# Products of zeros in the gaps of the opening, and measured landing times for the first loads

## The chip, the cores and the metric

The kernel runs on one core of one Trainium2 chip. The metric is the device time of one execution in microseconds (us). Several executions are timed; one more is recorded by the hardware profiler, and all rows below come from that one.

## What is computed

The reference is a linear attention with the feature map elu(x) + 1, followed by a mixture of four small networks whose outputs are added with weights that depend on the row.

```
q, k, v: [8 batches, 8 heads, 576 positions, 64]      float32
phi(x) = where(x > 0, x, exp(x) - 1) + 1
kv  = sum over s of phi(k)[s, d] * v[s, e]             per batch and head
z   = sum over s of phi(k)[s, d]
x   = (phi(q) @ kv) / (phi(q) . z + 1e-6)              -> 4608 rows x 512
p   = domain_probs / sum(domain_probs)                 4608 x 4
out = sum over e of p[:, e] * (relu(x @ w1[e]) @ w2[e])
w1: [4, 512, 1024], w2: [4, 1024, 512]                 float32
```

## The kernel before, in words

**Tiling.** A batch has 576 positions: 512 are handled as a block of four chunks of 128, and the remaining 64 of each batch are gathered as "rest" rows. Heads are taken in pairs, so a batch has four pairs (pr = 0 to 3), each 128 columns of x. For each pair ScalarE takes the exponential (ek, L469), VectorE makes the feature map from it (kqp, L453 and L454), TensorE transposes phi(q) (L481), ScalarE copies the transpose to SBUF (qT, L494), TensorE sums phi(k) times v (L512, with the denominators beside it in L514, and the rest rows in L520), ScalarE casts that sum to SBUF (kvz, L531 and L532), TensorE multiplies by it (L545, denominators in L547), and VectorE divides (reciprocal L552, product L553, which writes x).

**Stages.** In the opening, which is batch 0, the products of the first expert cannot start before x exists. `turn_x` transposes the x of a pair on TensorE (L668), and ScalarE copies it to `xt0` (L673, shown in the profile by its buffer's name, s). The first layer of expert 0 (`first_l1` and `mm1`, L678) then runs as soon as pieces of it can: the 128-row slices of w1 are called dc, 0 to 3, slice dc needs x of pair dc, and four banks are accumulated in parallel so that each slice is used as it comes. Its second layer is `mm2` (L688). The other three experts follow for batch 0, with the attention of batch 1 between them. From about 82 us on, the 64 units of the remaining batches run in a form with seven products instead of eight per pair of half blocks (`l1_seven`, L832, and `l2_unit`, L908), which needs sums of weight blocks that VectorE makes (`sums_w1`, L630, and `sums_w2`, L651). While these run, the attention of later batches is computed ahead.

**What sets the order.** The class `Plan` collects all operations with an engine, a duration, a priority and the data keys they read and write. `Plan.order` lays them out once, then `deadlines` replaces the priority of every operation that is not on TensorE by the latest time at which it may start (`late`), and the operations are laid out again. `lay_out` models the engines and one shared stream of transfers: a transfer has a time to move (`move`), a lead before it and a landing time after it. POOL's operations keep the order in which they are written. The order of instructions in the program, and so in every engine's queue, is that of the second layout. The hardware's engines then work through their queues in that order, and semaphores hold them where data or a PSUM bank isn't free.

**Loads.** `load_pair` issues the k, v and q of a head pair and `load_rest` those of the rest rows, both through `dma` (L261). The first pair and the k and v of the first rest rows are issued on the SP queue, all that follows in the opening on POOL: the pairs 1 to 3, then w1 and w2 of expert 0 (`load_w1`, `load_w2`), then those of the other experts.

**PSUM banks that matter here.** l2b1 receives the transposes of phi(q) of the opening in its first half (the 16-bit view's 512 columns are 256 columns of 32 bits). l2b2 receives the sums and the denominators. l2b3 receives the transposes of x, and `at` the products L545. `identh` is the identity matrix for transposes, made on POOL; `qTr` are two buffers for the transposed rest rows that VectorE sets to zero at the start.

Of the kernel before, what the change touches and what calls it, by code (L numbers as in the profile page):

```python
# [20 lines left out]
class Plan:  # L21
# [37 lines left out]
    def deadlines(self):  # L59
        ops = self.ops  # L60
        late = [o["start"] if o["eng"] == "PE" else BIG for o in ops]
        for n in range(len(ops) - 1, -1, -1):
            o = ops[n]
            for d in o["deps"]:
                x = ops[d]
                lat = self.HOP if x["eng"] != o["eng"] or x["move"] else 0.03
                if x["move"]:
                    lat += x["lead"] + x["move"] + self.LAND
                late[d] = min(late[d], late[n] - lat - x["dur"])
        for n, o in enumerate(ops):  # L70
            if o["eng"] != "PE":
                o["pri"] = late[n]

    def order(self):
# [59 lines left out]
def kernel(  # L134
# [10 lines left out]
    nc = tc.nc  # L145

    B, H, S, D = q.shape
    N, E = moe_domain_probs.shape
    _, Dm, F = moe_w1.shape

    P = 128
    NT = 512
    C = NT // P
    R = S - NT
    DE = D + 1
    DC = Dm // P
# [2 lines left out]
    HD = Dm // 2  # L159
    FH = F // 2  # L160
    NJ = N // NT
    T0, TU = 79.0, 6.4

    pl = Plan()
# [5 lines left out]
    def sb(name, shape, dt):  # L170
        return pc.tile(shape, dt, tag=name, name=name)
# [29 lines left out]
    qTr = [sb(f"qTr{i}", [P, DC, P], FP16) for i in range(2)]  # L201
# [6 lines left out]
    identh = s15h[:, 0:P]  # L208
# [22 lines left out]
    l2b = [pp.tile([P, 512], FP32, tag=f"l2b{i}", name=f"l2b{i}") for i in range(4)]  # L231
# [6 lines left out]
    def rot(key, n):  # L238
        i = cnt.get(key, 0)
        cnt[key] = i + 1  # L240
        return i % n
# [5 lines left out]
    def stage_keys(i):  # L247

        if i < 2:
            return ("st", i, 0), ("st", i, 1), ("st", i, 2)  # L250
        return ("xp", 0), ("xp", 1), ("u2", 0)
# [4 lines left out]
    def dma(queue, pri, out_, in_, w, move, r=(), hold=None, mark=None, after=0.0):  # L256

        eng = {"POOL": nc.gpsimd, "SP": nc.sync, "ACT": nc.scalar}[queue]

        def go():  # L260
            i = eng.dma_start(out=out_, in_=in_)  # L261
            if mark:
                last[mark] = i.ins.name
            if hold:
                tc.add_manual_dep(
                    i.ins,
                    last[hold],
                    mybir.DependencyInfo(
                        mybir.DependencyClass.Sync, mybir.DependencyReason.DATA
                    ),  # L270
                    reason="load order",
                )

        pl.add(
            queue,
            0.72 if queue == "POOL" else 0.5,
            pri,
            go,
            r=r + ((("mark", hold),) if hold else ()),
            w=w + ((("mark", mark),) if mark else ()),  # L280
            move=move,
            after=after,
        )
# [3 lines left out]
    def v16(i):  # L287

        flat = vss[i].rearrange("p h c d -> p (h c d)").bitcast(FP16)
        return flat[:, 0 : 2 * C * D].rearrange("p (h c d) -> p h c d", h=2, c=C)  # L290

    def load_pair(b, pr, queue, pri, after=0.0, hold=None):
        hs = slice(2 * pr, 2 * pr + 2)
        n = 3 if b < 2 else 2
        i = rot("stage%d" % n, n) if n == 2 else rot("stage3", 3)
        stage[b, pr] = i
        kk = stage_keys(i)
        vo = vss[i] if b or queue == "SP" else v16(i)
        parts = [(k, kqs[i][:, 0], kk[0]), (v, vo, kk[2]), (q, kqs[i][:, 1], kk[1])]
        if b == 0:  # L300
            parts[1:] = parts[:0:-1]
        for t, o, key in parts:
            if (b, pr, key) == (0, 0, kk[1]):
                load_rest(0, "SP", 0, parts=(0,))
            keys = (key, "v00") if (b, key) == (1, ("st", 1, 2)) else (key,)
            dma(queue, pri, o, t[b, hs, 0:NT].rearrange("h (p c) d -> p h c d", c=C), keys, 0.7,
                hold="w" if b == 2 else hold if key == kk[0] else None,
                mark="k0" if (b, pr, key) == (0, 0, kk[0]) else None, after=after)

    def load_rest(b, queue, pri, after=0.0, parts=(0, 1, 2)):  # L310
        par = b % 2
        rs = slice(par * R, par * R + R)
        for i in parts:
            t, o = ((k, kqr[rs, 0]), (v, vr[rs]), (q, kqr[rs, 1]))[i]
            dma(queue, pri, o, t[b, :, NT:S].rearrange("h s d -> s h d"), (("str", par, i),), 1.1,
                hold="w" if b in (2, 3) else None, after=after)

    def load_w1(e, dcs):
# [455 lines left out]

    units = [(j, s, e) for j in range(1, NJ) for s in range(2) for e in range(E)]
    U = lambda n: T0 + n * TU

    def prep(n):

        j, s, e = units[n]  # L780
        xi, ti = n % 2, n % 3
        xp, xT = xp_b[xi], xT_b[ti]
        pri = U(n) - 7.0
        for c in range(2):
            cc = 2 * s + c
            if j < NJ - 1:
                src, ps = x_b[j % 2][:, cc, :], p_nat[:, j, cc, e : e + 1]
                r = [("x", j % 2, pr, cc) for pr in range(DC)] + ["pnat" if j > 1 else "pnat0"]
            else:
                src, ps = xr_sb[:, cc, :], p_rest[:, cc, e : e + 1]  # L790
                r = [("xr", b, pr) for pr in range(DC) for b in (2 * cc, 2 * cc + 1)] + ["prest"]
            pl.add("ACT", 0.6, pri, lambda c=c, src=src, ps=ps: nc.scalar.activation(  # L792
                xp[:, c, :], src, AF.Copy, scale=ps), r=r, w=(("xp", xi, c),))
        pl.add("SP", 1.25, pri + 1, lambda: nc.sync.dma_start_transpose(
            out=xT.rearrange("p c k t -> p (c k) t"), in_=xp.rearrange("p c d -> p (c d)")),
            r=(("xp", xi, 0), ("xp", xi, 1)), w=(("xT", ti),), move=1.5, lead=0.2)
# [100 lines left out]
    def l2_unit(n):  # L897
# [88 lines left out]
        r = (O(0), O(2))  # L986
        if j < NJ - 1:
            dma("SP", p0 + 9, out_t[j][:, 2 * s : 2 * s + 2, :], ot, (), 1.5, r=r)
# [5 lines left out]
    def consts(i):  # L994
        nc.vector.memset(vps[i][:, :, :, D:DE], 1.0 / SX)
        nc.vector.memset(vprs[i][(1 - i) * R : (2 - i) * R], 0.0)
        nc.vector.memset(vprs[i][i * R : (i + 1) * R, :, D:DE], 1.0 / SX)
# [5 lines left out]
    pl.add("DVE", 0.4, 5, lambda: [nc.vector.memset(kvs[i], 0.0) for i in range(4)],  # L1003
           w=(("kvz", 0), ("kvz", 1), ("kvz", 2), ("kvz", 3)))
    pl.add("DVE", 0.8, 20, lambda: consts(1), w=(("vp", 1), ("vpr", 1)))
    for i in range(2):
        pl.add("DVE", 0.27, 26 + 10 * i, lambda i=i: nc.vector.memset(qTr[i], 0.0),
               w=[("qTr", i, pr) for pr in range(DC)])
    load_pair(0, 0, "SP", 0)
    load_rest(0, "SP", 0, parts=(1,))  # L1010
    load_pair(0, 1, "POOL", 0, hold="k0")
    load_pair(0, 2, "POOL", 0)
    rest_maps(0, True, 3, (0,))
    for pr in range(DC):
        if pr == 3:
            load_pair(0, 3, "POOL", 0)
            load_w1(0, range(DC))
            probs(0, 2, p5_b, ("p5",), "pnat0", 24)
            load_w2(0)
            load_rest(0, "POOL", 0, parts=(2,))  # L1020
        attention(0, pr, True, 2.5 + pr, 0.4, two=True)
        turn_x(pr, 4.9 + pr)
# [34 lines left out]
    def batch(b):  # L1057

        due = U(8 * (b - 1)) - 8
        for pr in range(DC):  # L1060
# [6 lines left out]
                rest_maps(b, False, t - 2)  # L1067
            attention(b, pr, False, t, 1.5)

    prep(0)  # L1070
    prep(1)
    for n in range(nu):
# [9 lines left out]
    with tc.manual_schedule(  # L1082
        engines={
            mybir.EngineType.PE,
            mybir.EngineType.Activation,
            mybir.EngineType.DVE,
            mybir.EngineType.Pool,
            mybir.EngineType.SP,
        }
    ):  # L1090
        todo = pl.order()
        for o in todo:
            o["fn"]()


# [28 lines left out]
```

## Time and profile before

| | |
|---|---|
| median of 4 runs | 498.97 us (497.71 to 499.8) |
| the profiled execution's own time | 499.8 us |
| its span | 498.0 us |
| TensorE busy | 481.1 us of the span (97%) |
| VectorE busy | 408.7 us (82%) |
| ScalarE busy | 366.6 us (74%) |
| POOL busy | 41.6 us (8%) |
| granted TensorE clock, mean | 0.998 |

A row of the timeline gives the start in us, the busy time in us, the engine, the line of the kernel, the operation, what it writes and reads, the size and the number of instructions merged into the row; in brackets stands how long the engine was idle before it and what ended that. PE is TensorE, ACT is ScalarE, DVE is VectorE. A row of waits names the waiting engine, the line that waited, what it waited for, the sum of the waiting time, how often, and the longest. A row of the chain gives a start, a duration and what was working then; the chain is followed back from the last instruction of the program. [...] what the products themselves show of the speed of the array is read from how far apart they start.

### The profile page before, as it was taken

The numbers are of one execution on the slowest core, as the hardware profiler recorded it, in microseconds if no ns is written. First come the engines' busy times: TensorE is split into PE (matmuls) and PEld (weight loads), VectorE is DVE, ScalarE is ACT, GpSimd is POOL, SyncE is SP. The second block draws the span as 40 slices with busy tenths as digits, with TensorE's granted clock in tenths as the row PEclk, the third lists the DMA queues.
The fourth block names the chain that finished last, engine by engine and source line by source line (L and its number), as shares of the span: only waits on it lengthen the run. The fifth ranks groups of instructions, "written<-read, shape, count | busy, mean of one in ns | idle before, by whom it ended". The sixth has DMA issues, their size and how long they took to land.

```text
span 498.0 us, 14872 instructions
## 1 busy us (share of the span) xinstructions
PE 481.1 (97%) x6040; PEld 426.1 (86%) x6040; DVE 408.7 (82%) x1033; ACT 366.6 (74%) x690; POOL 41.6 (8%) x67
## 2 busy tenths in 40 slices
PE   2899999999999999999999999999999999999995
PEld 2544456999999999999999999999999999999995
DVE  5668998988998999899988899889988675757664
ACT  5547658988987798769876988789766767676641
POOL 7656700000000000000000000000000000000000
PEclk9999999999999999999999999999999999999999
DMA  8999969948685686574656755657633233334221
GB/s 227 196 233 220 263 147 192 210 107 177 125 159 120 169 164 140 128 170 113 173 120 153 153 154 118 166 142 125 159 54 74 57 86 34 97 44 77 54 44 43
DMA packets 125573, 67.11 MB, mean 135 GB/s; under 512 B 95520, under 2 KB 119600, under 8 KB 125504
## 3 DMA queue, kind: packets, MB, share of 16 engines
q1 hardware_dynamic: 116112, 51.79, 48.4%
q0 software_dynamic: 9232, 14.10, 13.8%
q8 instruction: 47, 0.77, 0.7%
q10 hardware_dynamic: 160, 0.26, 0.1%
q14 instruction: 22, 0.18, 0.1%
HBM read 45.16 MB, written 9.44 MB: 110 GB/s over the span
## 4 chain that ended last, share of the span: by engine, by line
PE 93%; DMA 2%; ACT 2%; POOL 1%; DVE 1%; issue 0%; DVEq 0%
PE l1b L832 40%; PE l2b L908 38%; PE l1b L678 6%; PE l2b L688 6%; PE at L568 2%; PE at L517 1%; DMA w<-in_moe_w_dram 1%; POOL kq L261 1%; DMA kq<-in_k_dram 1%; ACT xp L792 0%; DVE ot L972 0%; ACT h L846 0%; PE at L520 0%; PE l2b L481 0%; POOL vs L261 0%
## 5 line engine op out<-in xcount | busy, mean ns | idle before, releaser
L832 PEld LDWEIGHTS <-w 128*128 128x128 f16 x2048 | 133.4, 98 | 5.1
L846 ACT ACTIVATE h<-l1b 128x512 f16<-128x512 f32 x128 | 76.8, 600 | 53.7 <-PE l1b L832 48.5
L908 PE MATMUL l2b<-w,h 128*128 128x256 f16 x768 | 114.9, 273 | 0.0
L908 PE MATMUL l2b<-t,s 128*128 128x256 f16 x768 | 114.3, 273 | 0.0
L832 PEld LDWEIGHTS <-w1x 128*128 128x128 f16 x1536 | 100.1, 98 | 3.9 <-issue 0.2
L908 PEld LDWEIGHTS <-s 128*128 128x128 f16 x1024 | 90.9, 98 | 6.6
L852 DVE CUSTOM_DVE_ANT_0 h<-l1b,p 128x512 f16<-128x512 f32 x64 | 44.1, 690 | 45.3 <-PE l1b L832 42.0
L792 ACT ACTIVATE xp<-x,p_nat 128x512 f16<-128x512 f16 x112 | 77.6, 721 | 0.9 <-DMA kqr<-in_q_dram 0.2
L832 PE MATMUL l1b<-xT,w 128*128 128x128 f16 x1024 | 78.1, 219 | 0.0
L832 PE MATMUL l1b<-xs,w 128*128 128x128 f16 x1024 | 78.1, 219 | 0.0
L832 PE MATMUL l1b<-xs,w1x 128*128 128x128 f16 x1024 | 77.9, 219 | 0.1
L908 PEld LDWEIGHTS <-h 128*128 128x128 f16 x768 | 67.4, 98 | 4.5
L894 DVE TENSOR_TENSOR s<-h 128x512 f16<-128x512 f16 x128 | 53.9, 421 | 2.1
L849 ACT COPY l1b<-l1b 128x512 f32<-128x512 f32 x64 | 36.7, 574 | 12.4 <-PE l1b L832 11.7
L849 ACT COPY u<-l1b 128x512 f32<-128x512 f32 x64 | 37.5, 586 | 11.1 <-PE l1b L832 10.9
L852 DVE CUSTOM_DVE_ANT_0 h<-l1b,u 128x512 f16<-128x512 f32 x64 | 43.8, 684 | 1.1 <-PE l1b L832 0.4
L849 ACT COPY p<-l1b 128x512 f32<-128x512 f32 x64 | 37.4, 584 | 8.9 <-PE l1b L832 7.2
L810 DVE TENSOR_TENSOR xs<-xT,xs 128x256 f16<-128x256 f16 x128 | 36.8, 288 | 3.4
L469 ACT ACTIVATE ek<-kq 128x512 f16<-128x512 f32 x60 | 37.9, 632 | 2.2 <-DMA kq<-in_k_dram 1.6
L832 PE MATMUL l1b<-xT,w1x 128*128 128x128 f16 x512 | 39.0, 219 | 0.0
L908 PE MATMUL l2b<-w,s 128*128 128x256 f16 x256 | 38.4, 273 | 0.0
L454 DVE TENSOR_TENSOR kqp<-ek,kqp 128x512 f16<-128x512 f16 x64 | 27.2, 425 | 6.0 <-ACT ek L469 1.7
(125 smaller groups left out, 568.8 us busy)
## 6 DMA issues: line engine op xcount, KB each, us to landing
w<-in_moe_w_dram POOLq DMA_DIRECT2D x32, 256.0 KB, 8.1
out_dram<-ot SPq DMA_DIRECT2D x16, 512.0 KB, 2.9
kq<-in_k_dram SPq DMA_DIRECT2D x25, 256.0 KB, 3.2
kq<-in_q_dram SPq DMA_DIRECT2D x25, 256.0 KB, 3.1
vs<-in_v_dram SPq DMA_DIRECT2D x25, 256.0 KB, 3.9
kq<-in_k_dram POOLq DMA_DIRECT2D x5, 256.0 KB, 7.2
kq<-in_q_dram POOLq DMA_DIRECT2D x5, 256.0 KB, 6.1
xT<-xp SPq DMA_TRANSPOSE x64, 3.2
```

The costliest lines, as they stand in the source:

```text
L454: nc.vector.tensor_tensor(out=o, in0=ek[:, i], in1=o, op=AO.min)
L469: pl.add("ACT", 0.55, pri + i * step, lambda i=i: nc.scalar.activation(ek[:, i], kq[:, i], AF.Exp), r=(sk[i],), w=(("ek", ei, i),))
L678: nc.tensor.matmul(out=bank, lhsT=w1_sb[e][:, dc, fj * P : (fj + 1) * P], rhs=xt0[:, dc, :], start=(dc == 0), stop=(dc == DC - 1),)
L688: nc.tensor.matmul(out=bank, lhsT=hts[ht[fj]][:, c * P : (c + 1) * P], rhs=w2_sb[e][:, fj, :], start=(fj == 0), stop=(fj == FC - 1),)
L792: pl.add("ACT", 0.6, pri, lambda c=c, src=src, ps=ps: nc.scalar.activation(xp[:, c, :], src, AF.Copy, scale=ps), r=r, w=(("xp", xi, c),))
L810: lambda o=o, a=a, b_=b_: tt(out=o, in0=a, in1=b_, op=AO.subtract),
L832: nc.tensor.matmul(out=bank[:, fc * P : (fc + 1) * P], lhsT=wt[:, kc, fc * P : (fc + 1) * P], rhs=r[:, kc, :], start=(start and fc == 0 an ...
L846: return lambda: nc.scalar.activation(o, bank, AF.Relu)
L849: return lambda: nc.scalar.copy(o, bank)
L852: return lambda: nc.vector._custom_dve(TENSOR_ADD_SAT, out=o, in0=bank, in1=t, s0=BIG, s1=0.0)
L894: pl.add("DVE", 0.36, U(n + 1) + d - 0.5, lambda i=i, a=a, b_=b_, alu=alu: tt(out=s4[:, i], in0=a, in1=b_, op=alu), r=r, w=(Q(i),))
L908: nc.tensor.matmul(out=l2b[bank][:, half * HD : (half + 1) * HD], lhsT=a[:, c, :], rhs=w[:, c], start=(opens and first and c == 0), stop=( ...
```

## The change

The change has three parts.

First, a function `keep_warm` issues one product on TensorE: the identity against 256 columns of `qTr[0]`, which holds zeros, written to the second half of bank l2b1, where nothing reads it. When the finished order is turned into instructions, each gap that the planner's layout leaves on TensorE before 22 us (`WARM`) is filled with as many such products as fit at 0.115 us each, less 0.1 us; in the first gap 28 (`COLD`) fewer are issued. In the built program there are 78: 43, 15, 4, 2, 3, 3 and 8 in the gaps from the first to the last.

Second, the setting to zero of `qTr[0]` is moved out of the plan to an earlier place, so that it stands in VectorE's queue ahead of the clearing of `kvs`.

Third, the planner's model gets other times for moving the first transfers of batch 0: 0.7, 1.2 and 0.95 us for the three parts of the first pair on SP in place of 0.7 each, 0.72 for the pairs on POOL, and 1.8, 0.7 and 0.7 for the rest rows in place of 1.1. The five first loads get negative priorities, which `deadlines` now leaves as they are. These numbers are in the model alone; what they alter is the order in which the planner puts the instructions. In the built program the five loads keep their order. TensorE's order is the same, apart from the zero products, until about 84 us; VectorE's and ScalarE's differ in a few places from about 24 and 37 us on; after 84 us all orders differ in places.

```diff
@@ Plan.deadlines
-            if o["eng"] != "PE":
+            if o["eng"] != "PE" and o["pri"] >= 0:
                 o["pri"] = late[n]
...
+    WARM, COLD = 22.0, 28
     T0, TU = 79.0, 6.4
@@ load_pair
             if (b, pr, key) == (0, 0, kk[1]):
-                load_rest(0, "SP", 0, parts=(0,))
+                load_rest(0, "SP", -8, parts=(0,))
             keys = (key, "v00") if (b, key) == (1, ("st", 1, 2)) else (key,)
-            dma(queue, pri, o, t[b, hs, 0:NT].rearrange("h (p c) d -> p h c d", c=C), keys, 0.7,
+            pri += queue == "SP" and not b
+            dma(queue, pri, o, t[b, hs, 0:NT].rearrange("h (p c) d -> p h c d", c=C), keys,
+                0.72 if queue == "POOL" or b else (0.7, 1.2, 0.95)[parts.index((t, o, key))],
@@ load_rest
-            dma(queue, pri, o, t[b, :, NT:S].rearrange("h s d -> s h d"), (("str", par, i),), 1.1,
+            dma(queue, pri, o, t[b, :, NT:S].rearrange("h s d -> s h d"), (("str", par, i),),
+                1.1 if b else (1.8, 0.7, 0.7)[i],
@@ the start of the program
-    for i in range(2):
-        pl.add("DVE", 0.27, 26 + 10 * i, lambda i=i: nc.vector.memset(qTr[i], 0.0),
-               w=[("qTr", i, pr) for pr in range(DC)])
-    load_pair(0, 0, "SP", 0)
-    load_rest(0, "SP", 0, parts=(1,))
+    nc.vector.memset(qTr[0], 0.0)
+    pl.add("DVE", 0.27, 36, lambda: nc.vector.memset(qTr[1], 0.0),
+           w=[("qTr", 1, pr) for pr in range(DC)])
+    load_pair(0, 0, "SP", -9)
+    load_rest(0, "SP", -7, parts=(1,))
...
+    def keep_warm():
+
+        nc.tensor.matmul(out=l2b[1][:, 256:512], lhsT=identh,
+                         rhs=qTr[0][:, 0:2].rearrange("p a t -> p (a t)"), start=True, stop=True)
@@ issuing the order
         todo = pl.order()
+        free = 0.0
         for o in todo:
+            if o["eng"] == "PE" and o["start"] < WARM:
+                gap = o["start"] - free
+                for _ in range(int((gap - 0.1) / 0.115) - (COLD if free == 0.0 else 0)):
+                    keep_warm()
+                free = o["start"] + o["dur"]
             o["fn"]()
```

## The prediction

> **What bounds the kernel now.** I read the page's busy table and slices first, then TensorE's waits, the chain in order of time, and last the timeline of the first 30 us, where the change lies.
>
> ```profile
> PE 481.1 (97%) x6040; PEld 426.1 (86%) x6040; DVE 408.7 (82%) x1033; ACT 366.6 (74%) x690; POOL 41.6 (8%) x67
> PE   2899999999999999999999999999999999999995
> ```
>
> TensorE is busy 97% and only the first two slices (12.45 us each) and the last are not full.
>
> ```profile
> PE l2b L481 <- DVE kqp L454: 7.2, 1, 7.2
> PE l2b L512 <- ACT vs L463: 1.2, 1, 1.2
> PE l2b L668 <- DVE x L553: 1.1, 2, 0.7
> PE at L545 <- ACT kvz L532: 1.0, 1, 1.0
> PE l1b L678 <- ACT s L673: 0.7, 1, 0.7
> ```
>
> These are all of TensorE's listed waits in the whole run: 11.2 us, the last at 24.29. After that it is fed to the end, so whatever brings the product at 24.29 forward brings the end forward, as long as its inputs keep up. That chain, in order of time, is led by transfers up to 16.93 (the weights w1 of expert 0) and by TensorE from there.
>
> ```profile
> 10.57 6.36 DMA w<-in_moe_w_dram
> ...
> 18.75 0.85 PE l1b L678 x2
> 19.61 0.43 PE l2b L481 x4
> ...
> 25.35 3.61 PE l1b L678 x16
> ```
>
> Here is the prize. Two 128x512 products take 0.85 us at 18.75, 0.43 each; sixteen take 3.61 us at 25.35, some 0.22 each. The timeline shows the switch at 21.54: the pair of products L545 and L547 needs 0.133 us before it and 0.083 after. The row PEclk stands at 9 throughout, so it does not show this. From 16.97 to 21.54 TensorE works without a gap at half speed: 4.57 us that could take about half.
>
> [...] half rate, and 4.57 us from the start of unbroken work to the switch. [...] the reciprocal L552 of pair 0 had its own sums at 11.57 but started at 12.33, when products of the next pair into the same bank had ended at 12.23.
>
> **The change, part by part.**
>
> *The zero products.* The built program's order has 78 of them, each 128x256, into the unused half of bank l2b1: 43 ahead of the first transposes (L481), 15 ahead of pair 0's L545, 4 ahead of turn_x of pair 0 (L668), 2 ahead of pair 1's L545, 3 ahead of pair 2's transposes, 3 ahead of turn_x of pair 1, 8 ahead of the dc=3 products of L678. A 256-column product costs, by half of the 512-column rows, 0.213 us at half clock and 0.109 at full.
>
> Their start: identity (POOL, done at 1.31) and the memset of qTr0, which moves up behind the memset that ends at 2.25 and takes 0.27; so about 2.55.
>
> Clock release: I take the trace's own 4.57 us, giving 7.1. [...]
>
> Now walk the queue with 7.1. Of 43 products 21 or 22 run slow, the rest fast: 2.55 + 21.4 x 0.213 + 21.6 x 0.109 = 9.5 [...]. The first transposes stood at 7.19; they move to 9.5. What is queued behind: ScalarE's copy of qT, 9.43, goes to 9.96. The 15 products come next and wait, by the bank, for that copy to end: 10.6, plus 15 x 0.109 = 12.25. L545 of pair 0 stood at 10.90. So pair 0's products end 1.35 us late less what the faster clock gives back (9 pairs at 0.05 here); its reciprocal goes from 12.33 to 13.2. Behind it ScalarE casts kvz (two casts, 0.45 in all) and then copies qT of pair 1, 13.9 to 14.5, and the 4 products wait for that: 14.55 + 0.44, so turn_x of pair 0 goes from 13.32 to 15.0. Add 0.22 for its own transposes, 0.22 for 2 products, 0.33 for pair 1's L545 group and 0.38 plus 0.17 of drain for pair 2's sums, which share the bank: they end at 16.3 instead of 15.15. Reciprocal, casts and the copy qT of pair 2 follow (0.1 + 0.25 + 0.45 + 0.6): 17.7 instead of 16.54. Then 3 products, 0.33: turn_x of pair 1 goes from 16.25 to 18.1, and the first L678 0.22 later, from 16.97 to 18.3. **So TensorE enters the dense stretch 1.35 us late.**
>
> From there everything runs at full clock and the loss is made good: up to the transposes of pair 3 (L481, 19.40) the same queue of one product, pair 2's sums, pair 3's sums and two products took 2.45 us and takes 0.22 + 0.33 + 0.38 + 0.43 = 1.36, giving 19.7; L545 of pair 3 comes at 20.95 instead of 21.54; its reciprocal at 21.5 (22.17); turn_x of pair 3 at 22.55 (23.23); the copy L673 at 23.0 (23.65); the dc=3 products at 23.65 instead of 24.29. The 8 products ahead of them, 0.87 us, lie under that copy (0.42 us from transposes to its start, 0.59 of its own, 0.05 after), so cost nothing; without that cover they would cost all 0.87. Sum: **-0.65 us**. [...] With all products taken out of the way and a clock that is up, it gives 22.3 (-2.0), limited by the elementwise work of pair 3 and by the norms.
>
> *Do inputs keep up?* POOL's queue issues each load when the one eight before it has landed, so its rows tell landings: w1 of expert 0 complete by 20.97, w2 of it by 26.7, w1 of expert 1 by 31.95. Expert 1's first product stands at 33.98, its dc=3 one 0.65 later; a gain of up to 2.6 us meets no load. None of the early POOL loads waits for TensorE. VectorE is near its limit from 33.3 to 79 (its waits for TensorE there sum to 1.3 us), but that stretch begins with a wait for L688 at 33.32 and so moves with it. I cost this at nothing; if the cover fails, the gain is lost at 81.84, where the first seven-product unit needs x of batch 1.
>
> *The planner's landing times and the fixed early priorities.* The order of the SP queue's first five loads is the same, and so is ScalarE's up to 35 us and TensorE's (zero products apart) up to about 84. VectorE takes the sums of w1 ahead of the first sum of w2; w1 had landed at 20.97, w2's first half by 24.1, so that is neutral to good. From 84 on all orders differ in places. TensorE shows no listed wait after 84 now, and 64 units x 14 products x 0.44 plus 24 attention pairs x 0.57 make 408 of the 410.8 us from 81.84 to 492.67: a better order can give back at most 2.8, a worse one has no such floor. I take 0, with -1.0 to +1.0 as ends.
>
> *Sum.* -0.65 + 0 against the profiled execution: 499.8 us (span 498.0 and 1.8 around it) would be 499.15. That execution is the slowest of the four; the median is 498.97, and I apply the difference to it: 498.3.
>
> **The rivals.**
>
> 1. *Half a gain (main).* As worked out: 498.3, own range 497.2 to 499.7. For it: the waits by bank and the queue in front of the transposes. Chance 0.50.
> 2. *The whole gain.* The clock is up before 6 us and the bank waits are shorter, or the new order takes up some of the 2.8 us. 2.0 us: 497.0 (496.2 to 497.5). Against it: the three groups that wait for the qT copies have to slip. Chance 0.30.
> 3. *Slower: the clock comes late.* [...] the 43 and 15 products run at 0.213 us in front of real work. All 43 slow end at 11.7. Break-even is at a release of about 8.4, a loss of 1.5 us at about 11.5 (501 at 12.5), and with no release before real work is dense the walk ends near 29, that is 503.7. For it: from 14.7 to 18.1 TensorE was over 80% busy in the trace of before and the clock was not released at 18.1. Against: the stream is unbroken. Chance 0.12.
> 4. *It does what it says and nothing comes of it:* VectorE's stretch from 40 to 79 does not move, TensorE waits at 81.84; 498.9. Against: that stretch begins with a wait for TensorE. Chance 0.08.
>
> **How the numbers follow.** About 0.3% (1.5 us) is what a measurement of this kernel can tell from no change. Faster than that: rival 2, 0.30, and a tail of the main case, 0.02. Slower: rival 3 less its mild part, and a bad order after 84: 0.12. Within: 0.56. Eight in ten lie from 496.5 to 500.0: this leaves out most of rival 3 and the best of rival 2.
>
> **What would show each step.** Right: zero products from about 2.5; their spacing falls from 0.21 to 0.11 near 7; first transposes near 9.5; pair 0's L545 near 12.2, released by ScalarE; the first L678 near 18.3 and at 0.22 each; the dc=3 products near 23.65. Wrong: L678 at or before 17.0 (rival 2); spacing of 0.21 up to 11 or later (rival 3); a TensorE wait near 81 (rival 4); equal times at 84 but not at the end (the order).

## The result, and the profile after

The changed kernel is slower: 500.34 us median (499.41 to 503.38) against 499.35 for the kernel before (497.71 to 500.45), ratio 1.0022 with a 95% interval of 1.0017 to 1.0028. That is 0.85 to 1.4 us lost, where 0.65 us was to be gained, and 500.34 lies just outside the range on record. The profiled execution took 500.21 us, its span is 498.4 (before: 499.8 and 498.0).

Lines of the kernel after are four higher than before: L481 is L485, L545 is L549, L668 is L672, L678 is L682, L747 is L751, L832 is L836, L852 is L856, L908 is L912. L1076 is the zero products.

The row of TensorE from the page's slices, kernel after. It answers to the row that began with 28:

```profile
PE   7899999999999999999999999999999999999995
```

The first slice is fuller, but it is filled with zeros. TensorE's waits in the whole run, kernel after (engine, line, what it waited for, us, times, longest):

```profile
PE l2b L1076 <- DVE qTr L1010: 2.6, 1, 2.6
PE l2b L1076 <- ACT qT L498: 2.4, 3, 1.2
PE l1b L836 <- DVE h L856: 0.3, 1, 0.3
PE at L572 <- DVE x L585: 0.2, 1, 0.2
```

The waits of before's opening, 11.2 us, are gone from the list or taken over by zero products. What is new is the third row: a product of the steady part waits for VectorE. No such row stood in the list before. The timeline of TensorE in the opening, kernel after:

```profile
2.55 7.62 PE L1076 MATMUL l2b<-qTr,s 128*128 128x256 f16 x43 [2.55 <-DVE qTr L1010]
10.01 0.39 PE L485 MATMUL l2b<-s,kqp 128*128 128x128 f16 x4
...
11.07 1.80 PE L1076 MATMUL l2b<-qTr,s 128*128 128x256 f16 x15 [0.29 <-ACT qT L498]
...
15.02 0.60 PE L1076 MATMUL l2b<-qTr,s 128*128 128x256 f16 x4 [1.22 <-ACT qT L498]
...
18.22 0.49 PE L1076 MATMUL l2b<-qTr,s 128*128 128x256 f16 x3 [0.89 <-ACT qT L498]
18.54 0.39 PE L672 MATMUL l2b<-s,x 128*128 128x128 f16 x4
18.76 0.38 PE L682 MATMUL l1b<-s,w 128*128 128x512 f16 x1
...
24.13 0.81 PE L682 MATMUL l1b<-s,w 128*128 128x512 f16 x3
```

The change does what it says. Three products take 0.49 us and fifteen 1.80, so one costs 0.109 at full clock. The 43 took 7.62, which fits about 27 of them at 0.213: the clock was released near 8.2. The dense stretch starts late (18.76 for 16.97) and at full clock, and the dc=3 products of L682 start at 24.13 instead of 24.29.

From there both kernels run alike up to the first seven-product unit, at 81.69 after and 81.84 before. At the end TensorE has lost: its last product ends at 493.31 after and 492.67 before. So a lead of 0.15 us at 82 is a lag of 0.64 at the end, and the loss lies in the steady part. Measured from the first product that reads w1x (82.13 after, 82.29 before) to TensorE's end, **the steady part** is 411.17 us after and 410.38 before.

The largest single piece of it is near 86 us. TensorE there, kernel after:

```profile
85.52 0.61 PE L836 MATMUL l1b<-xT,w 128*128 128x128 f16 x8
86.48 0.61 PE L836 MATMUL l1b<-xs,w 128*128 128x128 f16 x8 [0.35 <-DVE h L856]
```

Eight such products otherwise start 0.45 us after the eight before them; here it is 0.96. They wait for VectorE's L856 to empty their bank. In the kernel before, nothing waits there:

```profile
85.49 0.60 PE L908 MATMUL l2b<-w,h 128*128 128x256 f16 x4
85.93 0.61 PE L832 MATMUL l1b<-xs,w1x 128*128 128x128 f16 x8
```

VectorE's timeline ahead of L852 (L856 after), first before, then after:

```profile
83.06 0.74 DVE L747 SCALAR_TENSOR_TENSOR ot<-l2b,p_nat,ot 128x512 f32<-128x512 f32 x1
83.72 0.41 DVE L810 TENSOR_TENSOR xs<-xT 128x512 f16<-128x512 f16 x1
84.06 0.74 DVE L747 SCALAR_TENSOR_TENSOR ot<-l2b,p_nat,ot 128x512 f32<-128x512 f32 x1
84.76 0.69 DVE L852 CUSTOM_DVE_ANT_0 h<-l1b,u 128x512 f16<-128x512 f32 x1
```

```profile
82.32 0.73 DVE L751 SCALAR_TENSOR_TENSOR ot<-l2b,p_nat,ot 128x512 f32<-128x512 f32 x1
82.98 0.41 DVE L375 TENSOR_SCALAR kqpr<-kqr 64x512 f16<-64x512 f32 x1
83.49 0.42 DVE L376 TENSOR_TENSOR kqpr<-ek,kqpr 64x512 f16<-64x512 f16 x1
83.83 1.40 DVE L751 SCALAR_TENSOR_TENSOR ot<-l2b,p_nat,ot 128x512 f32<-128x512 f32 x2
85.15 0.67 DVE L856 CUSTOM_DVE_ANT_0 h<-l1b,u 128x512 f16<-128x512 f32 x1
```

VectorE is idle for no more than 0.11 us at a time in either stretch; it is a matter of what is queued ahead. Counted over the program, the new order puts one L751 more (0.73 us) and one pair L375 and L376 more (0.83) ahead of the first L856, and one L814 less (0.41). That makes 1.15 us. About 0.6 of it fell into idle time that VectorE still had in the kernel before, in gaps of 0.49 and 0.48 us ahead of its instructions at 78.14 and 80.75. The rest stayed: L856 starts 3.02 us after the first w1x product (85.15 less 82.13) instead of 2.47 (84.76 less 82.29). The difference, 0.55, is about the gap that TensorE shows (0.96 less 0.45). This is the **knot** in the experiments below.

### The profile page after: what moved, and what is told of

Same layout as the page of the kernel before. It is cut to its first block, busy times and chain, and to the rows that moved or that the text cites. A ratio compares the mean times of both kernels' runs of the same rounds, so it can differ in the third digit from the quotient of the medians.

```text
span 498.4 us, 15028 instructions
## 1 busy us (share of the span) xinstructions
PE 487.7 (98%) x6118; PEld 432.0 (87%) x6118; DVE 410.6 (82%) x1033; ACT 367.3 (74%) x690; POOL 41.5 (8%) x67
## 4 chain that ended last, share of the span: by engine, by line
PE 96%; DVE 2%; ACT 1%; issue 1%; DVEq 0%
PE l1b L836 39%; PE l2b L912 38%; PE l1b L682 5%; PE l2b L692 5%; PE l2b L1076 2%; PE at L572 2%; PE at L521 1%; DVE h L856 1%; DVE ot L976 0%; DVE ot L751 0%; ACT qT L498 0%; PE at L524 0%; PE l2b L485 0%; PE at L549 0%; PE l2b L672 0%
## 5 line engine op out<-in xcount | busy, mean ns | idle before, releaser
L836 PEld LDWEIGHTS <-w 128*128 128x128 f16 x2048 | 133.3, 98 | 5.6 <-issue 0.5
L912 PE MATMUL l2b<-w,h 128*128 128x256 f16 x768 | 114.9, 273 | 0.0
L912 PE MATMUL l2b<-t,s 128*128 128x256 f16 x768 | 114.2, 273 | 0.0
L836 PEld LDWEIGHTS <-w1x 128*128 128x128 f16 x1536 | 100.0, 98 | 3.7 <-issue 0.4
L912 PEld LDWEIGHTS <-s 128*128 128x128 f16 x1024 | 91.0, 98 | 6.7
L856 DVE CUSTOM_DVE_ANT_0 h<-l1b,p 128x512 f16<-128x512 f32 x64 | 44.1, 689 | 42.5 <-PE l1b L836 40.2
L836 PE MATMUL l1b<-xs,w 128*128 128x128 f16 x1024 | 78.0, 219 | 0.3 <-DVE h L856 0.3
L836 PE MATMUL l1b<-xT,w 128*128 128x128 f16 x1024 | 78.1, 219 | 0.0
L836 PE MATMUL l1b<-xs,w1x 128*128 128x128 f16 x1024 | 77.9, 219 | 0.1
L912 PEld LDWEIGHTS <-h 128*128 128x128 f16 x768 | 67.4, 98 | 4.6
L856 DVE CUSTOM_DVE_ANT_0 h<-l1b,u 128x512 f16<-128x512 f32 x64 | 43.7, 684 | 2.1 <-PE l1b L836 1.4
L853 ACT COPY u<-l1b 128x512 f32<-128x512 f32 x64 | 37.5, 585 | 10.8 <-PE l1b L836 10.6
L853 ACT COPY l1b<-l1b 128x512 f32<-128x512 f32 x64 | 36.7, 574 | 11.7 <-PE l1b L836 11.0
L853 ACT COPY p<-l1b 128x512 f32<-128x512 f32 x64 | 37.4, 584 | 7.8 <-PE l1b L836 7.1
L814 DVE TENSOR_TENSOR xs<-xT,xs 128x256 f16<-128x256 f16 x128 | 36.9, 288 | 4.4 <-PE at L524 0.5
L836 PE MATMUL l1b<-xT,w1x 128*128 128x128 f16 x512 | 39.0, 219 | 0.0
L912 PE MATMUL l2b<-w,s 128*128 128x256 f16 x256 | 38.4, 273 | 0.0
```

What stands on the lines that cost most here:

```text
L814: lambda o=o, a=a, b_=b_: tt(out=o, in0=a, in1=b_, op=AO.subtract),
L836: nc.tensor.matmul(out=bank[:, fc * P : (fc + 1) * P], lhsT=wt[:, kc, fc * P : (fc + 1) * P], rhs=r[:, kc, :], start=(start and fc == 0 an ...
L853: return lambda: nc.scalar.copy(o, bank)
L856: return lambda: nc.vector._custom_dve(TENSOR_ADD_SAT, out=o, in0=bank, in1=t, s0=BIG, s1=0.0)
L912: nc.tensor.matmul(out=l2b[bank][:, half * HD : (half + 1) * HD], lhsT=a[:, c, :], rhs=w[:, c], start=(opens and first and c == 0), stop=( ...
```

## The experiments

Twelve kernels were run, each timed in five rounds beside the kernel before. In the table "dc=3" is the start of the dc=3 products of L678, "w1x" that of the first product which reads w1x, and "steady" the time from there to TensorE's end, each from the one profiled execution; the ratio is to the kernel before as it ran beside it on the same chip, so it can differ a little from that of two medians in the table.

| kernel | median us | ratio (95%) | dc=3 | w1x | steady |
|---|---|---|---|---|---|
| before | 499.35 | 1 | 24.29 | 82.29 | 410.38 |
| after | 500.34 | 1.0022 (1.0017 to 1.0028) | 24.13 | 82.13 | 411.17 |
| e1 new order, no zeros | 500.54 | 1.0023 (1.0016 to 1.0031) | 23.73 | 81.73 | 411.15 |
| e2 old order, zeros | 499.17 | 1.0001 (0.9993 to 1.0010) | 23.48 | 81.48 | 410.18 |
| e3 old order, zeros in l1b2 | 498.37 | 0.9989 (0.9978 to 0.9999) | 22.55 | 82.14 | 410.17 |
| e4 old order, first zeros alone, early | 499.47 | 1.0004 (0.9995 to 1.0013) | 24.54 | 82.54 | 410.17 |
| e5 old order to 120, then new | 499.92 | 1.0013 (1.0005 to 1.0020) | 23.44 | 81.44 | 410.48 |
| e6 new order to 120, then old | 500.24 | 1.0022 (1.0013 to 1.0031) | 24.52 | 82.52 | 410.80 |
| e7 new landing times, due times later | 500.14 | 1.0015 (1.0006 to 1.0025) | 23.00 | 81.00 | 410.54 |
| e8 old landing times, due times earlier | 500.44 | 1.0017 (1.0009 to 1.0024) | 25.06 | 83.08 | 410.95 |
| e9 old order, memset early | 499.32 | 1.0002 (0.9992 to 1.0012) | 23.72 | 81.72 | 410.24 |
| e10 old order, zeros early and in l1b2 | 498.78 | 0.9995 (0.9982 to 1.0008) | 22.78 | 80.98 | 410.16 |
| e11 old order, first 43 alone, in l1b2 | 499.51 | 1.0006 (0.9999 to 1.0014) | 23.83 | 81.84 | 410.16 |
| e12 after, zeros in l1b2 | 500.35 | 1.0021 (1.0010 to 1.0032) | 22.60 | 82.88 | 411.18 |

### The two halves: e1 and e2

e1 leaves out the zero products and keeps the new landing times, priorities and memset:

```diff
-                for _ in range(int((gap - 0.1) / 0.115) - (COLD if free == 0.0 else 0)):
-                    keep_warm()
```

> The changed kernel with its planner's landing times, priorities and early memset, but without any of the 78 zero products, so its order of instructions is the changed one and the opening runs at half clock as before. Theory A (two halves: the zero products cost the opening about as much as the faster clock gives, and the new order of the steady stage costs 0.5 to 0.8 us): 0.4 to 0.9 us slower than before (ratio 1.0008 to 1.0018), with the TensorE wait for VectorE's L856 near 86 us still there. Theory B (the products alone cost the 1.0 us): ratio 0.9995 to 1.0005. Theory C (the order alone costs it): ratio 1.0018 to 1.0026.

e2 is the kernel before with the memset moved and the same 78 zero products ahead of the same TensorE operations:

```diff
+        zeros = {1: 43, 3: 15, 6: 4, 7: 2, 9: 3, 10: 3, 29: 8}
+        nth = 0
         for o in todo:
+            if o["eng"] == "PE":
+                nth += 1
+                for _ in range(zeros.get(nth, 0)):
+                    keep_warm()
             o["fn"]()
```

> The kernel before with its own planner and order, the memset of qTr0 moved up, and the same 78 zero products at the same seven places of TensorE's queue. Theory A: 0.1 to 0.6 us slower (ratio 1.0002 to 1.0012), dc=3 products of L678 between 23.6 and 24.8, no new TensorE wait near 86 us. Theory B: 0.9 to 1.3 us slower (ratio 1.0018 to 1.0026). Theory C: ratio 0.9995 to 1.0005.

Theory C fits: the order alone has the whole loss (1.0023), the zeros alone move nothing that can be measured (1.0001). The interval of e2 still leaves room for the few tenths of theory A, but the steady part says the same without it: 411.15 with the new order, 410.18 with the old one. The knot is in e1 as well, in TensorE's waits:

```profile
PE l1b L836 <- DVE h L856: 0.4, 1, 0.4
```

TensorE was 0.56 us earlier at 82 in e1 than before (81.73 for 82.29), and L856 started at 84.76 in both. So it is not that TensorE runs ahead of VectorE: in e2 TensorE is earlier still (81.48) and has no wait there.

### Where in the order: e5 and e6

Both make the two plans in the kernel and join them. Operations that both plans start before 120 us are issued in one order, the others in the other:

```diff
+        def key(n):
+            early = max(sa[n], sb[n]) < 120.0
+            return (0, first[n], n) if early else (1, then[n], n)
+        for n in sorted(range(len(pl.ops)), key=key):
```

> No zero products. Both plans are made in the kernel (with the old and with the new landing times); operations that both start before 120 us on their own clock are issued in the old order, all later ones in the new order. Measured so far: the new order alone costs 1.1 us (ratio 1.0023) and TensorE's extra stalls between its matmuls are 0.95 us from 80 to 100 against 0.24 in the old order, and later about 1.15 against 1.05. Theory 'knot at the entry' (the cost sits where the opening meets the first units, mainly the 0.5 us at 85.5 where products of L836 wait for VectorE to empty a PSUM bank): without that stretch the cost goes, ratio 0.9998 to 1.0007. Rival 'spread' (the new order is a little worse everywhere): the larger part stays, ratio 1.0012 to 1.0020.

> No zero products; the counterpart: operations that both plans start before 120 us are issued in the new order, all later ones in the old order. Knot at the entry: the whole cost comes with that stretch, ratio 1.0013 to 1.0023, with L836 waiting for VectorE's L856 near 86 us. Spread: 1.0003 to 1.0008.

e6, with the new order up to 120 us alone, has the knot and a ratio of 1.0022, as the theory of the knot said. TensorE, kernel e6 (its L841 and L861 are L836 and L856):

```profile
86.87 0.61 PE L841 MATMUL l1b<-xs,w 128*128 128x128 f16 x8 [0.46 <-DVE h L861]
```

But e5, without that stretch, is not free of cost: 1.0013, where the theory of the knot said 0.9998 to 1.0007; it lies in the range of its rival. The two ratios together come to more than e1's 1.0023, within their intervals; the steady parts are closer and add up: against 410.2 for the old order (the middle of its seven executions) e6 has 0.6 us more and e5 0.3, together e1's 0.95. So about two thirds of the traced loss sit at the entry, one third in later places of 0.1 to 0.3 us each.

### Why the order is worse: e7, e8 and e9

The new landing times (in the model the 0.72 us holds for the pairs of later batches as well) put the plan's opening about 1.07 us later, while the steady units' due times are counted from a constant, T0. e7 is e1 with T0 moved by as much; e8 is the kernel before with T0 moved the other way.

```diff
-    T0, TU = 79.0, 6.4
+    T0, TU = 80.07, 6.4
```

(77.93 in e8.)

> No zero products; the new order's landing times, with T0, from which all due times of the steady units are counted, put 1.07 us later (80.07 for 79.0), by as much as the new landing times move the plan's opening. Theory 'misfit' (a later opening against due times that stayed is what squeezes the entry): the cost goes, ratio 0.9995 to 1.0007. Theory 'draw' (any shift of the planner's times makes another interleaving, good or bad by about 1 us, and the size or direction of the shift says nothing): anywhere from 0.998 to 1.003, and as likely as not outside that.

> The kernel before, old landing times, with T0 put 1.07 us earlier (77.93 for 79.0): the same misfit from the other side. Misfit: as slow as the new order, ratio 1.0015 to 1.003, with a wait of L832's products for VectorE near 86 us. Draw: anywhere from 0.998 to 1.003; 0.9995 to 1.0007 would speak against misfit.

The knot follows the misfit. With T0 moved along (e7) it is gone: L857, its L856, starts 2.47 us after the first w1x product, as before, and TensorE lists no wait after 75 us. With T0 moved away in the old kernel (e8) the queue ahead of L853, its L852, is longer by the same instructions as in the kernel after, and L853 starts 3.02 us after the first w1x product. The same holds in all fourteen kernels: 3.02 in after, e1, e6, e8 and e12, 2.47 in the others. VectorE again holds TensorE up at the entry, though not where it was expected: products of the second layer (its L909 is L908) wait for a sum:

```profile
87.36 0.61 PE L909 MATMUL l2b<-t,s 128*128 128x256 f16 x4 [0.34 <-DVE s L895]
```

The time does not follow as far: e7 still has 1.0015, a miss of its range. In its trace other gaps came in the place of the knot, spread from 130 to 390 us, and its steady part is 0.34 us over the old order's. Every shift of the planner's times gave another interleaving, and none of those tried was as short as the old one's 410.2. That is what the rival called a draw, but not a blind one: the planner's own layout has e7 close to the old order and after and e8 some 1 us behind it (see the section on the prediction).

In e1, e5 and e7 the medians rose by 0.2 to 0.5 us more than the steady parts. e9, with the old order from end to end and the memset moved, asks whether the memset does that:

> No zero products; both plans are made in the kernel as in the two kernels with a seam, and the old order is issued from end to end. What differs from the kernel before is the place of the memset of qTr[0] and nothing else. In those two kernels and in the one with later due times, TensorE's steady part (first product of L832 to its end) was 0.1 to 0.6 us longer than before's, and the medians were 0.6 to 0.9 us longer: 0.3 to 0.5 us more than the steady part explains. Theory 'noise' (the rest lies within the intervals): ratio 0.9994 to 1.0006. Rival 'memset' (the earlier memset delays VectorE's opening and all kernels with it): 1.0006 to 1.0012.

1.0002 is what noise would give; its interval (0.9992 to 1.0012) does not shut out the rival. The rest lies within the intervals of all three, and these runs say no more on it. e9 shows one thing more: TensorE's, VectorE's, ScalarE's and POOL's orders in its trace are those of the kernel before but for the memset, with the new priorities and the old landing times. So the landing times make the new order, and the negative priorities do nothing by themselves.

### What the zero products are worth: e3, e10, e11, e4 and e12

In the kernel after three groups of fillers wait for ScalarE's copies of qT, 2.4 us in all; they write bank l2b1, which holds the transposes that are copied. e3 is e2 with the first 70 in l1b2, which nothing else uses before 16 us:

```diff
-                    keep_warm()
+                    keep_warm(l2b[1] if nth == 29 else l1b[2])
```

> As e2, but the first 70 products write to bank l1b2, which nothing reads or writes before the first layer, so that none of them waits for ScalarE's copy of qT; the last 8 stay in l2b1. If the waits by bank are what eats the gain of the clock, the dc=3 products of L678 come 1.0 to 1.5 us earlier than in e2, at 22.3 to 23.3, and the run is 1.0 to 1.6 us faster than e2 and 0.5 to 1.5 us faster than before (ratio 0.997 to 0.999). If instead the 43 products ahead of the first transposes are what eats it, e3 is within 0.4 us of e2.

TensorE lists no wait for those copies in e3. dc=3 came 0.93 us earlier than in e2, at 22.55, and the ratio, 0.9989, is the only one below 1 by its interval, if barely. In its profiled execution the lead was gone at 82 us (82.14). But that execution, at 499.75 us, was the fourth slowest of 22 (median 498.37), so others probably kept the lead. e12 makes the same edit in the kernel after:

> The changed kernel with one edit: its first 70 zero products write PSUM bank l1b2, which is free, in place of l2b1, where they wait for ScalarE's copies of qT; order and counts are unchanged. Theory 'the zeros' own bank waits eat the gain' (the same edit in the old order gave 0.9989 against 1.0001, with wide intervals): the fillers start at 10.0 behind the first K^T V, first L682 at 17.2, dc=3 at 22.5 to 22.9, and with the new order's 1.1 us the ratio is 1.0008 to 1.0014, still slower than before. Rival 'the front does not set the time' (with the bank free the loads and VectorE take over between 40 and 74 us): dc=3 as early, ratio 1.0018 to 1.0025, as the changed kernel.

dc=3 came 1.53 us earlier than in the kernel after, and the time did not move that can be measured (1.0021 for 1.0022), as the rival said; the interval of e12, 1.0010 to 1.0032, does not shut the theory out. In the table, the first w1x product follows 58.0 us behind dc=3 in every kernel whose dc=3 starts at 23.0 or later. In e10 it is 58.2, in e3 59.6, in e12 60.3. In these executions the front ends last down to about 23; ahead of that something else can. In e12 it is seen in TensorE's waits and in ScalarE's timeline:

```profile
PE l1b L682 <- ACT h L714: 1.6, 1, 1.6
```

```profile
38.72 0.63 ACT L473 ACTIVATE ek<-kq 128x512 f16<-128x512 f32 x1 [1.09 <-DMA kq<-in_k_dram]
40.26 0.63 ACT L469 CAST vp<-vs 128x512 f16<-128x512 f32 x1 [0.91 <-DMA vs<-in_v_dram]
41.73 0.63 ACT L473 ACTIVATE ek<-kq 128x512 f16<-128x512 f32 x1 [0.85 <-DMA kq<-in_q_dram]
42.27 1.07 ACT L714 ACTIVATE h<-l1b 128x512 f16<-128x512 f32 x2
```

Here ScalarE waits for the loads of batch 1, and the L714 that empties the bank of L682 stands behind them in its queue. These loads did not come earlier with the front. They came late in this execution: k of batch 1 landed at 38.70 us, the latest of the fourteen traces (37.15 in after, 36.57 in e2). How much of a lead they take in a usual execution is therefore not shown.

e10 joins the free bank with an earlier start: the memset of qTr[0] goes first in VectorE's queue, and 34 zeros start at 1.36.

> The old order; 34 zero products from about 1.4 us (memset of qTr[0] first in VectorE's queue) and then the same fillers, all but the last eight in PSUM bank l1b2, which no earlier work holds. It joins what two kernels showed apart: an earlier start of the zeros (clock free at about 6, first transposes at 8.8) and no wait on ScalarE's copies of qT (ratio 0.9989). Theory 'TensorE's front sets the opening': dc=3 products at 21.5 to 22.2, ratio 0.9975 to 0.9988. Rival 'loads and VectorE take over between 40 and 74 us': dc=3 as early, but what is gained over the 22.55 of the kernel with the bank alone is given back, ratio 0.9985 to 0.9993.

It met the loads even sooner. The first L679 (its L678) waits for w1, TensorE's timeline of e10:

```profile
17.36 0.39 PE L679 MATMUL l1b<-s,w 128*128 128x512 f16 x1 [0.83 <-DMA w<-in_moe_w_dram]
```

dc=3 was at 22.78, later than either theory said, and 0.9995 cannot be told from no change. In e3 and e12 the first such product waits for w1 as well, until 17.18 and 17.22. This too differs between executions: that part of w1 landed between 15.38 (e1) and 17.39 us (e8).

e4 (34 zeros from 1.36, no fillers, in l2b1) and e11 (43 zeros, no fillers, in l1b2) ask whether the fillers are needed:

> The kernel before with its own order and 34 zero products in one group only, ahead of the first transposes; the memset of qTr0 is VectorE's first instruction, so they start at about 1.4 us and are over by 8.6 at the latest. If the clock that they release stays up through the sparse work between 9 and 17 us without further products, the dc=3 products of L678 come at about 22.3 and the run is 1.5 to 2.2 us faster than before (ratio 0.9955 to 0.997). If the clock falls back, L678 at 17.0 is at 0.43 us each again and the run is within 0.4 us of before.

> The old order; only the 43 zero products ahead of the first transposes, in bank l1b2; none of the fillers after. Theory 'the fillers keep the clock': as with 34 zeros alone, transposes of pair 1 near 11.6 us run at half clock again (0.6 us for eight against 0.4), dc=3 at 24 to 24.6, ratio 1.0000 to 1.0006. Rival 'once is enough': the clock stays, dc=3 at about 22.5, ratio 0.9985 to 0.9993.

They are. e4's TensorE:

```profile
1.36 5.54 PE L1072 MATMUL l2b<-qTr,s 128*128 128x256 f16 x34 [1.36 <-POOL s masks.py:199]
8.01 0.40 PE L481 MATMUL l2b<-s,kqp 128*128 128x128 f16 x4 [1.11 <-DVE kqp L454]
...
11.63 0.63 PE L481 MATMUL l2b<-s,kqp 128*128 128x128 f16 x4
```

Four transposes take 0.40 us at full clock and 0.63 at half. The clock was up by the end of the zeros and down again at 11.6. In e11 it was up to 14.2, longer than expected, and down from there: turn_x of pair 1 took 0.61 at 16.25. Both then entered the dense stretch at half clock as the kernel before does, with dc=3 at 24.54 and 23.83.

The kernel nearest to a gain is e3, whose interval ends at 0.9999. Two things were not measured: the second L751 of the pair at 83.8 taken behind L856 in the new order, which would test the knot by itself, and e3 a second time.

## Why the prediction was wrong

**The step that failed** is the one on the planner's new order after 84 us: "I take 0, with -1.0 to +1.0 as ends". It measured 0.8 us by the steady parts of the two traces, 1.0 against the middle of the old order's seven executions, and 1.1 by the ratio of e1: at the upper end or past it. The argument for 0 saw that a worse order "has no such floor" and that TensorE listed no wait after 84, and still took the middle. What it left out was in the profile: from 80.75 us to L852 VectorE is idle for no more than about 0.1 us at a time, so what a new order puts ahead of L852 beyond the idle time before that is paid for. That TensorE had no wait there before meant that the old order fitted there, not that there was room to spare: the orders of e1, e6 and e8 have the wait.

It was in the planner too. `Plan.order`, computed from the kernels as they stand, ends TensorE's last operation at 491.30 us before and at 493.42 after: 2.12 later, where the opening accounts for 1.07. The other 1.05 is a loss on the planner's own clock, and most of it lies at the entry: TensorE's gaps of over 0.1 us there, from 79 us on, sum to 0.47 us in the plans of before and e7, to 1.21 in that of after and 1.19 in that of e8. Less the shift of the opening, the plans of e7, after and e8 end 0.21, 1.05 and 1.31 us later than that of before; the steady parts measured 0.34, 0.97 and 0.75 over 410.2. The term could have been worked out before anything was run.

**The zero products' walk was right.** Release was taken at 7.1, an estimate from the 4.57 us in the one trace of before; how far it could lie from that was not shown there. The rows of zeros give about 8.2 for after, 6.9 for e2 and e3, 7.4 for e11 and e12, and the granted clock in these traces begins there (8.24, 6.89, 6.89, 7.39 and 7.48). The walk gives 24.2 at 8.2 and 23.5 at 6.9; measured were 24.13 and 23.48. The wait of the fillers for the qT copies, the late start of the dense stretch (18.3 predicted, 18.76 after, 18.11 in e2) and its full clock came as worked out. The eight products ahead of dc=3 cost next to nothing: it starts 0.09 us after the copy L677 ends, 0.05 without them (e1).

**The -0.65 us was measured from a late execution.** With no zeros the release of the clock differs from one execution to the next: dc=3 lay at 24.29, 23.73, 23.44, 24.52, 23.00, 25.06 and 23.72 in before, e1 and e5 to e9, a mean of 23.97. In the same order the granted clock begins at 21.66, 20.61, 19.72, 22.11, 19.31, 22.88 and 20.46. The 58.0 us from dc=3 to w1x and the 5.3 or 5.4 us behind TensorE's end are the same in all seven, so a late release is paid for in full. Against the mean of 23.97 the zeros of after and e2, 24.13 and 23.48, are worth some 0.2 us, with too few executions to tell that from nothing. The text saw that the profiled execution was the slowest of four, and applied its difference to the median in spite of it; the half speed that it counted was in part what made it slow. -0.2 and +1.0 make +0.8; measured is +0.85 to +1.4. The 0.3 us in the middle are no more than the two terms are uncertain by: by their ratios, e1 lost 1.1 us and e2 0.05.

**"A gain of up to 2.6 us meets no load" was wrong,** without weight for this result. With dc=3 at 22.6, 1.7 us ahead of before's, the loads of batch 1 hold ScalarE up in e12's trace, and in e3, e10 and e12 the first L678 waits until 17.2 to 17.4 for w1 of expert 0.

**The rivals.** Rival 2, the whole gain of 2.0 us, was not reached with the bank waits taken out either: the interval of e3 allows up to 1.1 us, that of e10 up to 0.9, and the traces of e3, e10 and e12 show waits for loads. Rival 3, slower because of a late clock, was the right sign for the wrong reason: release at 8.2 lay within its break-even of 8.4. The forecast's last sentence named the case that came true: equal times at 84 but not at the end. It had no price of its own and shared a chance of 0.12.

## What to carry to other kernels

When a change alters the numbers that a list scheduler plans with, price the new order as a risk of its own: here it cost 1.0 us, the zero products gained nothing that could be measured, and none of the five other orders that were run cost less than 0.3 us of TensorE's time. Compare the scheduler's own end time and gaps for the two orders first. Look for the engine that has no gap where the stages meet, and count what the new order puts ahead of its first urgent instruction. A gain taken from a profiled execution should be measured against several: the state that it removes (here a clock released late) may be what set that execution apart.

## What the runs showed of the hardware that was not expected

In e4 and e11 the clock fell back although TensorE, once it had begun, was never idle for more than 1.6 us at a time. In e4 the unbroken work ended at 6.9 us and in e11 at 10.4; groups of real products of 0.4 to 1.1 us followed, with gaps of 0.4 to 1.6 us between them. The granted clock in the traces fell to half at 11.61 and 14.22, 6.83 us after its release in both, and rose again at 21.85 and 21.05, 10.24 and 6.83 us later. The row PEclk, which stood at 9 in the kernels before and after, shows this; kernel e4:

```profile
PEclk9699999999999999999999999999999999999999
```

The half rate ahead of the first release is not in that row: in the kernel before it stands at 9 from the start, while products of 512 columns start 0.43 us apart up to 21.54 and 0.22 after. The mean granted clock of every timed execution shows the fall as well: 0.988 to 0.991 in all 14 of e4, 0.988 to 0.992 in 20 of the 22 of e11, and 0.996 or more in the other kernels.

From the end of the unbroken work to the fall TensorE was busy 35% of the time in e4 (6.90 to 11.61) and 48% in e11 (10.36 to 14.22). In after, e2, e3, e10 and e12, which have the fillers, the clock held; in after TensorE was busy 70% of the time from 10.78, where its unbroken work ended, to the first L682 at 18.76. What decides it these runs do not show.

From the first zero product to the release it took 3.4 us (e4), 3.6 (e10), 4.3 (e2), 4.8 (e11), 4.9 (e12) and 5.7 (after), all of it unbroken zeros.
